# First loads of a fused attention and feed-forward kernel: keys and first queries first, and products of ones on TensorE while they load

## Chip, core and metric

The kernel runs on one core of a Trainium2 chip. The metric is the device time of one execution in microseconds. The time before is the median of 9 runs; beside it stands one profiled execution, from which all times of single instructions come.

## The reference

Attention over 8 batches of 8 heads, 576 tokens of 64 channels, in which a score counts only if it lies within tau of its row's maximum; the result, with heads side by side, goes through a gated feed-forward block. All is float32.

```
scores = (q @ k^T) / 8
scores = where(scores >= max(scores) - tau, scores, -1e9)
attn   = exp(scores - max) / (sum + 1e-9)
x      = (attn @ v) as (8*576, 512)
g      = x @ w_gate                       # 512 x 1536
out    = (g * sigmoid(g) * (x @ w_val)) @ w_out   # 1536 x 512
```

Weights arrive as they are in HBM; the kernel keeps w_gate and w_val in `wgv` and w_out in `wo`.

## The kernel before

**Work units.** Two heads make a pair; `NP` = 4 pairs make a batch, 32 pairs are done in all. A pair's queries and keys come as `[128, 18, 32]` tiles of 576 columns (`qraw`, `kraw`), are turned by VectorE's 32x32 transpose (`prepare`, L783 and L784) and multiplied. Queries are scaled first (L248, on GpSimd) with `scl`, which is computed from tau (L97 to L100).

**Segments.** The main loop runs over segments, numbered from 0, and in each over tiles of 128 queries. Segments 0 to 3 take the first two tiles (256 queries, `QA`) of pairs 0 to 3. Segments 4 to 7 take the other tiles (two of 128 and one of 64) of pairs 3, 0, 1, 2. From segment 8 on each segment is a whole pair in another layout. For segments 4 to 7 the remaining 320 queries of pairs 0 to 3 are transposed apart: pair 0's and pair 3's at L789 in `prepare`, pairs 1's and 2's at L856, at the end of the first two tiles of segment 4 (list `later`).

**A tile.** TensorE makes the scores (L311); VectorE takes the row maxima (L338); ScalarE takes exponentials (L345); VectorE cuts by tau and sums (L349), then L373 and L374 give the reciprocal. In segments 0 to 3 ScalarE scales an identity by it (L385), and TensorE turns the tile by multiplying with that (`flip`, L417, L420). In segments 4 to 7 the tile is scaled itself, head 0 on ScalarE (L357) and head 1 on GpSimd (L355), and TensorE transposes it (L415, L422). ScalarE copies the turned tile from PSUM (L423, L428); one tile later TensorE multiplies it with the values (`attend_tile`, L443).

**Weights.** A weight piece is loaded (`fetch_weights`) into a landing place, split by ScalarE (`split_weights`, L193, L194) and joined by VectorE (L200, L204, L207) and GpSimd (L209) in `join_weights`: 24 pieces, usually one in a tile, and a place can be loaded anew once its join is done. `need(n)` joins at once what products need.

**Feed-forward products.** They start in segment 4 and are dealt out between the attention steps: `pace` works out how many fit, `fill` issues them (gate L505 `pg`, value L505 `pv`).

**Order.** The schedule is manual: each engine, and each engine's DMA queue, works through its instructions in program order. SyncE's queue (SP) issues nearly all loads, ScalarE's the keys of pairs 0 and 1. The tile pool `ld` has one buffer each for `qraw` and `kraw`; pairs 1 and 2 use parts of `extra` instead. In segments 0 to 3 the next pair but one is fetched after `prepare`; from segment 4 on `fetch_qk(seg["i"] + 1)` stands in each segment's first tile, ahead of the steps that cut and scale that tile:

```python
            if x == 0 and n >= NP:
                fetch_qk(seg["i"] + 1)
            next(go)
```

Pair 4 is fetched in segment 2, since `n < NP` there and pair 3 is already loaded.

Of the kernel before, what the change touches and what calls it, by code (L numbers as in the profile page):

```python
# [10 lines left out]
F32 = mybir.dt.float32  # L11
U32 = mybir.dt.uint32
U64 = mybir.dt.uint64
AF = mybir.ActivationFunctionType
ALU = mybir.AluOpType
# [4 lines left out]
def kernel(  # L20
# [30 lines left out]
    nc = tc.nc  # L51
    P = 128
    B, H, S, D = q.shape
    NP = H // 2
# [3 lines left out]
    G = 32  # L58
    NG = P // G
    NJ = S // G  # L60
# [6 lines left out]
    TC = 256  # L67
    XB = 5
# [5 lines left out]
    QA = TA * P  # L74
    SCALE = 1.0 / float(D) ** 0.5
    assert 2 * D == P and NCC == NP and D == 2 * G and S - SM == 2 * G and SM % TC == 0 and B % BT == 0 and QA == TC

    const = ctx.enter_context(tc.tile_pool(name="const", bufs=1))
# [14 lines left out]
    cut = const.tile([P, 1], F32, name="cut")  # L93
    cap = const.tile([P, 1], F32, name="cap")
    scl = const.tile([P, 1], F32, name="scl")
    nc.sync.dma_start(out=tau_s, in_=tau.partition_broadcast(P))
    nc.vector.tensor_scalar(out=scl, in0=tau_s, scalar1=0.0, scalar2=SCALE, op0=ALU.is_ge, op1=ALU.mult)  # L97
    nc.vector.tensor_scalar(out=cap, in0=tau_s, scalar1=0.0, scalar2=2e38, op0=ALU.is_ge, op1=ALU.mult)
    nc.vector.tensor_scalar(out=cap, in0=cap, scalar1=-1e38, scalar2=None, op0=ALU.add)
    nc.vector.scalar_tensor_tensor(out=cut, in0=tau_s, scalar=-1.0, in1=cap, op0=ALU.mult, op1=ALU.min)  # L100


    sums = deque(const.tile([P, 4, 3], F32, name=f"sums{i}") for i in range(4))
    for x in sums:
        nc.vector.memset(x[:, :, 2], 1e-9)
    minus2 = const.tile([P, 1], F32, name="minus2")
    nc.vector.memset(minus2, -2.0)
    vall = const.tile([P, 2 * NJ * D], F32, name="vall")


# [4 lines left out]
    ident = pall.rearrange("p n s -> p (n s)")[:, free:free + P]  # L115
    make_identity(nc, ident)
    arenas = [pall[:, 0:NR, :], pall[:, NR - 2:, :]]

    wgv = const.tile([P, 2, NCC, DFF], F32, name="wgv")

# [49 lines left out]
    def fetch_weights(n=1):  # L170
        for _ in range(n):
            if not wpieces or wpieces[0][2] in used:
                return
            dst, srcs, place = wpieces.popleft()
            used.add(place)
            m = 2 if len(srcs) == 2 else nf
            to = places[place].bitcast(U64).rearrange("p (m n) -> p m n", m=m)
            if len(srcs) == 1:
                nc.sync.dma_start(out=to, in_=srcs[0])
            else:  # L180
                for x, src in enumerate(srcs):
                    nc.sync.dma_start(out=to[:, x, :], in_=src)
            fetched.append((dst, place))
# [43 lines left out]

    def load_qk(i):
        b, hp_ = divmod(i, NP)
        raws = []  # L230

        free = {1: 0, 2: 1}.get(i)
        for name, src, order in (("q", q, "(j r) (e d) -> e r j d"), ("k", k, "(j r) (e d) -> e r j d" if b == 0 else "(r j) (e d) -> e r j d")):
            if free is None:
                raw = ld.tile([P, NJ, G], F32, name=f"{name}raw")
            else:
                n = 2 * free + len(raws)
                raw = extra[:, n * S:(n + 1) * S].rearrange("p (j d) -> p j d", d=G)
            queue = nc.scalar if i < 2 and name == "k" else nc.sync

            for js in [slice(0, QA // G), slice(QA // G, NJ)] if i == 0 and name == "q" else [slice(0, NJ)]:
                for g in range(NG):
                    h, e = divmod(g, 2)
                    queue.dma_start(out=raw[g * G:(g + 1) * G, js],
                                    in_=src[b, 2 * hp_ + h].rearrange(order, r=G, d=G)[e][:, js])
            raws.append(raw.rearrange("p j d -> p (j d)"))
        for cs in [slice(0, QA), slice(QA, S)] if i == 0 else [slice(0, S)]:
            nc.gpsimd.tensor_scalar(out=raws[0][:, cs], in0=raws[0][:, cs], scalar1=scl, scalar2=None, op0=ALU.mult)  # L248
        return raws

    def load_v(seg):
        b, hp_ = divmod(seg["i"], NP)
        src = v[b, 2 * hp_:2 * hp_ + 2]
        if seg["halved"]:
            half = seg["i"] % 2
            vr = vall[:, half * NJ * D:(half + 1) * NJ * D].rearrange("p (h j d) -> p h j d", h=2, d=D)
            for a in range(2):
                for c in range(2):
                    nc.sync.dma_start(out=vr[(2 * a + c) * G:(2 * a + c + 1) * G].rearrange("r h j d -> r h (j d)"),
                                      in_=src.rearrange("h (r c j) d -> c r h (j d)", c=2, j=NK)[c])  # L260
        else:
            own = vall[:, hp_ * S:(hp_ + 1) * S]
            vr = own[:, 0:2 * KT * D].rearrange("p (h t d) -> p h t d", h=2, d=D), own[:, 2 * KT * D:]
            for h in range(2):
                nc.sync.dma_start(out=vr[0][:, h], in_=src[h, 0:KM].rearrange("(t p) d -> p t d", p=P))
                nc.sync.dma_start(out=vr[1][h * D:(h + 1) * D], in_=src[h, KM:S])
        seg["v"] = vr
# [493 lines left out]
        return rate  # L761

    raws = {}
    kept = {}
    later = []

    def fetch_qk(i):
        if i < NPAIR and i not in raws and i not in kept:
            raws[i] = load_qk(i)

    def prepare(seg):

        i = seg["i"]
        if i in kept:
            seg.update(kept[i])
            return
        qr, kr = raws[i]
        kept[i] = None
        qT = qkp.tile([P, S], F32, name="qT")
        if i < NP:  # L780
            kT = pall[:, 4 + i, :]
            rest = flat[:, i * (S - QA):(i + 1) * (S - QA)]
            nc.vector.transpose(out=kT, in_=kr)  # L783
            nc.vector.transpose(out=qT[:, 0:QA], in_=qr[:, 0:QA])  # L784

            later.append((rest, qr[:, QA:S]))
            if i == 1 or i == NP - 1:
                to, fr = later.pop(0 if i == 1 else -1)
                nc.vector.transpose(out=to, in_=fr)  # L789
            kept[i] = {"kT": kT, "qT": rest, "q0": QA}  # L790
        else:
            kT = qkp.tile([P, S], F32, name="kT")
            nc.vector.transpose(out=kT, in_=kr)
            nc.vector.transpose(out=qT, in_=qr)
        seg.update(kT=kT, qT=qT, q0=0)

    def give(n):
# [2 lines left out]
            left[0] += cost(u)  # L800
        gains[n] = (gains[n][0], 0)

    fetch_qk(0)
    prepare(segs[0])
    fetch_qk(1)
    fetch_weights(2)
    load_v(segs[0])
    fetch_weights(2)
    prev, last = None, iter(())
    for n, seg in enumerate(segs):  # L810
        if NP <= n < 2 * NP:
            seg["v"] = segs[seg["i"]]["v"]
        for x, t in enumerate(seg["tiles"]):
            go = scores(seg, t)
            next(go)
            next(last, None)
            attends = prev is not None and x == 1
            products = iter(())
            attend_tile()
            next(go)  # L820
            next(last, None)
            flip()
            if n == NP and x == 0:
                attend_tile()
                give(n - 1)
            if n == 2 * NP and x == 1:
                give(n - 1)
            if attends and n > 2 * NP:
                if prev["i"] % NP == 0:
                    need(NW)  # L830
                    start_batch(prev["i"] // NP)
                products = attend(prev)
            part = pace(n, x) / 2
            more = len(split)
            if n or x:
                split_weights()
                fetch_weights(2)
            if x == 0 and n >= NP:
                fetch_qk(seg["i"] + 1)
            next(go)  # L840
            double = t == NT and NP <= n < NP + 2
            if more and not double:
                join_weights()
            fill(part)
            next(go)
            fill(part)
            if double:

                join_weights(2)
                split_weights()  # L850
                fetch_weights(2)
            gates()
            last = go
            if n == NP and later:
                to, fr = later.pop(0)
                nc.vector.transpose(out=to, in_=fr)  # L856
            if attends and n > 2 * NP:
                next(products)
                next(products)
                give(n - 1)  # L860
            if attends and seg["halved"]:
                load_v(seg)
            if x == 0 and 0 < n < NP:
                load_v(seg)
            if x == len(seg["tiles"]) - 2 and n + 1 < len(segs):
                prepare(segs[n + 1])
                if n < NP:
                    fetch_qk(segs[n + 1]["i"] + 1)
        prev = seg
    next(last)  # L870
    next(last)
# [40 lines left out]
```

## Time and profile before

| what | us |
|---|---|
| median of 9 runs (lowest, highest) | 1514.29 (1512.86, 1515.15) |
| the profiled execution: its own time | 1514.79 |
| its span | 1512.7 |
| TensorE busy in the span | 1480.6 |
| VectorE busy | 994.8 |
| ScalarE busy | 726.4 |
| GpSimd busy | 642.6 |
| first scores start | 7.94 |
| scores of segments 0 to 3 (two tiles each) start | 7.94, 12.98; 20.63, 26.10; 32.16, 38.40; 45.01, 52.81 |
| segment 4's first scores start | 58.33 |

Span times count from the first instruction. In a line of the timeline the first number is the start, the second the length in us, then come engine, source line, operation, what is written from what, shape, count, and in brackets the idle time before it and who ended it. SPq and ACTq are the DMA queues of SyncE and ScalarE. A 32-bit product of 256 columns shows as two records.

### The profile page before, as it was taken

To read this page: it belongs to the slowest core of one execution; us is meant where nothing else is said; L and a number is where in the kernel's file an instruction comes from. 1 tells how busy PE (TensorE), PEld (TensorE's weight loads), DVE (VectorE), ACT (ScalarE), POOL (GpSimd) and SP (SyncE) were. 2 spreads that over 40 slices of the span, in tenths; PEclk is the share of its full clock that TensorE was granted. 3 is DMA by queue.
4 is the path that set the end of the run, shared out by engine and by line. 5 is a ranking of instruction groups with operands and counts; after the bars stand their busy time and mean duration, and the time that the engine had idled before them with its cause. 6 is when DMAs were issued, how large, how long until landed. Compare 5 with 4: busy or idle time off the path is not lost. (4 is left out here: it accounts for less than half of the span.)

```text
span 1512.7 us, 31439 instructions
## 1 busy us (share of the span) xinstructions
PE 1480.6 (98%) x11784; PEld 1123.1 (74%) x11784; DVE 994.8 (66%) x3038; ACT 726.4 (48%) x2157; POOL 642.6 (42%) x638
## 2 busy tenths in 40 slices
PE   7999899999999999999999999999999999999999
PEld 5777664477777777787777777777777777888887
DVE  6878988777777777747767666776666767512212
ACT  5787665555455555434545444454544454311110
POOL 3355543367454535336444444543545353500000
PEclk9999999999999999999999999999999999999999
DMA  8542411211112111112111111212110120000000
GB/s 192 149 147 92 96 35 39 54 33 32 47 33 47 33 25 33 40 28 45 35 27 29 25 47 33 46 33 47 33 35 13 46 48 16 1 15 1 15 14 15
DMA packets 176871, 66.91 MB, mean 44 GB/s; under 512 B 159696, under 2 KB 159696, under 8 KB 176720
## 3 DMA queue, kind: packets, MB, share of 16 engines
q1 hardware_dynamic: 169552, 56.45, 16.5%
q0 software_dynamic: 2432, 7.87, 1.4%
q8 instruction: 93, 1.52, 0.4%
q10 hardware_dynamic: 4736, 0.59, 0.3%
q14 instruction: 58, 0.48, 0.1%
HBM read 55.44 MB, written 9.44 MB: 43 GB/s over the span
## 5 line engine op out<-in xcount | busy, mean ns | idle before, releaser
L355 POOL TENSOR_SCALAR pall<-pall,ri 128x288 f32<-128x288 f32 (+1 forms) x260 | 265.2, 1029 | 345.3 <-DVE ri L365 308.8
L505 PE MATMUL pv<-xall,wgv 128*128 128x256 f32 x1728 | 405.0, 383 | 3.0 <-ACT pall L423 2.7
L505 PE MATMUL pg<-xall,wgv 128*128 128x256 f32 x1728 | 403.3, 383 | 0.2 <-ACT pall L423 0.2
L505 PEld LDWEIGHTS pv<-xall,wgv 128*128 128x128 f32 x1728 | 324.8, 191 | 68.5 <-issue 22.3
L505 PEld LDWEIGHTS pg<-xall,wgv 128*128 128x128 f32 x1728 | 324.0, 190 | 64.9 <-issue 22.0
L326 DVE TENSOR_REDUCE mx<-sc 128x2 f32<-128x576 f32 x252 | 180.6, 751 | 237.6 <-PE sc L303 236.8
L349 DVE SCALAR_TENSOR_TENSOR pall<-sc,th,pall 128x288 f32<-128x288 f32 (+1 forms) x540 | 258.1, 528 | 31.5 <-ACT pall L345 31.5
L345 ACT ACTIVATE pall<-sc,nm 128x288 f32<-128x288 f32 (+1 forms) x540 | 236.4, 510 | 0.6
L341 ACT ACTIVATE th<-nm,cut 128x4 f32<-128x4 f32 (+1 forms) x140 | 41.6, 297 | 383.6 <-DVE nm L330 383.6
L537 POOL TENSOR_TENSOR ht<-ht,gt 128x512 f32<-128x512 f32 x84 | 107.0, 1274 | 193.5 <-DVE ht L525 109.8
L394 DVE STREAM_TRANSPOSE pall<-pall 128x576 f32<-128x576 f32 x252 | 181.3, 754 | 2.8 <-POOL pall L355 2.8
L603 PE MATMUL po<-wo,ht 128*128 128x256 f32 x768 | 177.6, 382 | 0.0
L303 PE MATMUL sc<-kT,qT 64*32 64x288 f32 x4032 | 158.4, 411 | 11.3 <-DVE pall L349 9.9
L603 PEld LDWEIGHTS po<-wo,ht 128*128 128x128 f32 x768 | 144.9, 190 | 26.2 <-issue 6.0
L525 DVE SCALAR_TENSOR_TENSOR ht<-tn,pv 128x512 f32<-128x512 f32 x102 | 69.9, 685 | 132.3 <-PE pv L505 119.1
L357 ACT ACTIVATE pall<-pall,ri 128x288 f32<-128x288 f32 (+1 forms) x264 | 132.9, 553 | 0.0
L279 ACT COPY sums<-sums 32x4 f32<-32x4 f32 (+1 forms) x560 | 108.5, 194 | 50.0 <-DVE pall L349 38.6
L518 ACT ACTIVATE tn<-pg 128x512 f32<-128x512 f32 x108 | 64.9, 600 | 139.8 <-PE pg L505 133.0
L469 PE MATMUL xa<-pall,vall 64*64 64x288 f32 x2016 | 128.7, 405 | 0.0
L303 PEld LDWEIGHTS sc<-kT,qT 64*32 64x32 f32 x4032 | 58.9, 106 | 88.9 <-issue 60.9
L469 PEld LDWEIGHTS xa<-pall,vall 64*64 64x64 f32 x2016 | 74.5, 133 | 50.5 <-ACT sums L279 3.6
L621 POOL TENSOR_TENSOR ht<-ht,xall 128x256 f32<-128x256 f32 x48 | 34.1, 728 | 156.3 <-PE po L603 155.1
(101 smaller groups left out, 1329.5 us busy)
## 6 DMA issues: line engine op xcount, KB each, us to landing
vall<-in_v_dram SPq DMA_DIRECT2D x112, 144.0 KB, 3.3
qraw<-in_q_dram SPq DMA_DIRECT2D x116, 72.0 KB, 2.4
kraw<-in_k_dram SPq DMA_DIRECT2D x116, 72.0 KB, 2.8
out_dram<-ob POOLq DMA_DIRECT2D x28, 256.0 KB, 3.1
wo<-in_moe_w_gate_dram SPq DMA_DIRECT2D x16, 384.0 KB, 3.7
wo<-in_moe_w_val_dram SPq DMA_DIRECT2D x16, 384.0 KB, 4.3
xall<-in_moe_w_out_dram SPq DMA_DIRECT2D x5, 768.0 KB, 4.6
wo<-in_moe_w_out_dram SPq DMA_DIRECT2D x3, 768.0 KB, 4.5
```

Source lines behind the costliest of these rows:

```text
L279: nc.scalar.copy(out, in_[:, :, 0])
L303: nc.tensor.matmul(ps[g * G:(g + 1) * G, h, 0:SH], qT[hs, col + a * G:col + (a + 1) * G], kT[hs, c * SH:(c + 1) * SH], start=True, stop=True)
L326: nc.vector.tensor_reduce(out=mx[:, 2 * x:2 * x + 2, 0], in_=tile_[:, :, 0:SH], axis=AX.X, op=ALU.max, negate=True)
L345: nc.scalar.activation(ps[x], scs[x], AF.Exp, bias=nm[:, x:x + 1])
L349: nc.vector.scalar_tensor_tensor(out=ps[x], in0=scs[x], scalar=th[:, x:x + 1], in1=ps[x], op0=ALU.is_ge, op1=ALU.mult, accum_out=sm[:, x, ...
L355: nc.gpsimd.tensor_scalar(out=ps[x], in0=ps[x], scalar1=ri[:, x:x + 1], scalar2=None, op0=ALU.mult)
L357: nc.scalar.activation(ps[x], ps[x], AF.Copy, scale=ri[:, x:x + 1])
L394: nc.vector.transpose(out=p, in_=p)
L469: nc.tensor.matmul(xa[a][h * D:(h + 1) * D, at:at + n * G].rearrange("d (i q) -> d i q", q=G), vr[rs, h, j, :], p[rs, lo:lo + n, j, :], st ...
L505: nc.tensor.matmul(ps[:, i], wgv[:, mat, c, (f + i) * P:(f + i + 1) * P], x[:, c, cs], start=(c == 0), stop=(c == NCC - 1))
L537: eng.tensor_tensor(out=hts[x], in0=hts[x], in1=gt, op=ALU.mult)
L603: nc.tensor.matmul(ps, h(f), w[:, f, :], start=(f == 0), stop=(f == NF2 - 1))
```

## The change

- **Loads of the first four pairs.** Keys come first, then only the first 256 queries; each is four DMAs. For pairs 0 and 1 two of the four go on SP's queue and two on ScalarE's. Tau is loaded on ScalarE's queue behind pair 0's keys. Values of pair 0 are loaded ahead of pair 2 and of the weights, and pairs 2 and 3 are fetched before the main loop.
- **Rests.** The other 320 queries are loaded and scaled in the first tiles of segments 1 (pairs 3 and 0), 2 (pair 1) and 3 (pair 2).
- **Scaling.** Pair 0's first queries are scaled by VectorE, after its key transpose.
- **Places.** Pair 3's tiles are in `xall` instead of the `ld` buffers. Pair 4, next to use those, is now fetched by the line shown above, in segment 4's first tile; there the last reader of pair 0's `qraw`, the transpose of its rest, stands at the end of the same tile (`later` holds pairs 0, 1 and 2, one in each tile of segment 4).
- **Products of ones.** `run_idle(6)` issues six 128x128 by 128x256 products before everything else and six after the first tile's scores.
- **Weights.** The first piece is split in segment 1's first tile instead of segment 0's second, so joins 1 to 8 are one tile later.
- **A one-element exponential** stands ahead of ScalarE's first real work.

```diff
-    nc.sync.dma_start(out=tau_s, in_=tau.partition_broadcast(P))
-    nc.vector.tensor_scalar(out=scl, in0=tau_s, ...)
...
+    ones = pall[:, 2 * NR - 4, 0:TC]
+    nc.vector.memset(ones, 1.0)
+    def run_idle(n):
+        ps = ps_f.tile([P, 512], F32, name="idle", tag="psf")[:, 0:TC]
+        for _ in range(n):
+            nc.tensor.matmul(ps, ones[:, 0:P], ones, start=True, stop=True)
...
+        places_ = {1: extra[:, 0:2 * S], 2: extra[:, 2 * S:4 * S], 3: xall[:, XB * XW:XB * XW + 2 * S]}
...
+        def load(name, js, queues):
+            src, order = srcs[name]
+            for g in range(NG):
+                h, e = divmod(g, 2)
+                queues[g // 2].dma_start(out=tiles[name][g * G:(g + 1) * G, js],
+                                         in_=src[b, 2 * hp_ + h].rearrange(order, r=G, d=G)[e][:, js])
+        def scale(cs):
             nc.gpsimd.tensor_scalar(out=raws[0][:, cs], in0=raws[0][:, cs], scalar1=scl, ...)
+        if i < NP:
+            queues = [nc.sync, nc.scalar if i < 2 else nc.sync]
+            load("k", slice(0, NJ), queues)
+            if i == 0:
+                nc.scalar.dma_start(out=tau_s, in_=tau.partition_broadcast(P))
+            load("q", slice(0, QA // G), queues)
+            if i == 0:
+                nc.vector.tensor_scalar(out=scl, in0=tau_s, ...)
...
+            else:
+                scale(slice(0, QA))
+            def load_rest():
+                load("q", slice(QA // G, NJ), [nc.sync] * 2)
+                scale(slice(QA, S))
+            more_loads.append(load_rest)
+        else:
+            for name in "qk":
+                load(name, slice(0, NJ), [nc.sync] * 2)
+            scale(slice(0, S))
...
             nc.vector.transpose(out=kT, in_=kr)
+            if i == 0:
+                nc.vector.tensor_scalar(out=qr[:, 0:QA], in0=qr[:, 0:QA], scalar1=scl, ...)
             nc.vector.transpose(out=qT[:, 0:QA], in_=qr[:, 0:QA])
             later.append((rest, qr[:, QA:S]))
-            if i == 1 or i == NP - 1:
-                to, fr = later.pop(0 if i == 1 else -1)
+            if i == NP - 1:
+                to, fr = later.pop()
                 nc.vector.transpose(out=to, in_=fr)
...
+    run_idle(6)
     fetch_qk(0)
     prepare(segs[0])
     fetch_qk(1)
+    nc.scalar.activation(junk, minus2, AF.Exp)
+    load_v(segs[0])
+    fetch_qk(2)
     fetch_weights(2)
-    load_v(segs[0])
+    fetch_qk(3)
     fetch_weights(2)
...
             next(go)
+            if not n and not x:
+                run_idle(6)
             next(last, None)
...
-            if n or x:
+            if 0 < n < NP and x == 0:
+                if n == 1:
+                    more_loads.rotate(1)
+                    more_loads.popleft()()
+                more_loads.popleft()()
+            if n:
                 split_weights()
                 fetch_weights(2)
...
                 prepare(segs[n + 1])
-                if n < NP:
-                    fetch_qk(segs[n + 1]["i"] + 1)
```

More of the change, by code (lines that the diff above doesn't have):

```diff
@@ L95 @@
     scl = const.tile([P, 1], F32, name="scl")
-    nc.sync.dma_start(out=tau_s, in_=tau.partition_broadcast(P))
[L97 to L100, printed above, removed]
     sums = deque(const.tile([P, 4, 3], F32, name=f"sums{i}") for i in range(4))
@@ L107 @@
     nc.vector.memset(minus2, -2.0)
+    junk = const.tile([P, 1], F32, name="junk")
     vall = const.tile([P, 2 * NJ * D], F32, name="vall")
@@ L229, in load_qk @@
         b, hp_ = divmod(i, NP)
[L230 to L235, printed above, removed]
-            else:
[L237 to L246, printed above, removed]
@@ L247, in load_qk @@
-        for cs in [slice(0, QA), slice(QA, S)] if i == 0 else [slice(0, S)]:
-            nc.gpsimd.tensor_scalar(out=raws[0][:, cs], in0=raws[0][:, cs], scalar1=scl, scalar2=None, op0=ALU.mult)
+        tiles = {}
+        places_ = {1: extra[:, 0:2 * S], 2: extra[:, 2 * S:4 * S], 3: xall[:, XB * XW:XB * XW + 2 * S]}
+        srcs = {"q": (q, "(j r) (e d) -> e r j d"),
+                "k": (k, "(j r) (e d) -> e r j d" if b == 0 else "(r j) (e d) -> e r j d")}
+        for x, name in enumerate("qk"):
+            if i in places_:
+                tiles[name] = places_[i][:, x * S:(x + 1) * S].rearrange("p (j d) -> p j d", d=G)
+            else:
+                tiles[name] = ld.tile([P, NJ, G], F32, name=f"{name}raw")
@@ new lines, in load_qk @@
+        raws = [tiles[name].rearrange("p j d -> p (j d)") for name in "qk"]
+        def load(name, js, queues):
[5 more added lines that the diff above has]
+        def scale(cs):
+            nc.gpsimd.tensor_scalar(out=raws[0][:, cs], in0=raws[0][:, cs], scalar1=scl, scalar2=None, op0=ALU.mult)
@@ new lines, in load_qk @@
+        if i < NP:
[5 more added lines that the diff above has]
+            if i == 0:
+                nc.vector.tensor_scalar(out=scl, in0=tau_s, scalar1=0.0, scalar2=SCALE, op0=ALU.is_ge, op1=ALU.mult)
+                nc.vector.tensor_scalar(out=cap, in0=tau_s, scalar1=0.0, scalar2=2e38, op0=ALU.is_ge, op1=ALU.mult)
+                nc.vector.tensor_scalar(out=cap, in0=cap, scalar1=-1e38, scalar2=None, op0=ALU.add)
+                nc.vector.scalar_tensor_tensor(out=cut, in0=tau_s, scalar=-1.0, in1=cap, op0=ALU.mult, op1=ALU.min)
+            else:
[8 more added lines that the diff above has]
+            scale(slice(0, S))
@@ L763 @@
     raws = {}
+    more_loads = deque()
     kept = {}
@@ L783, in prepare @@
             nc.vector.transpose(out=kT, in_=kr)
+            if i == 0:
+                nc.vector.tensor_scalar(out=qr[:, 0:QA], in0=qr[:, 0:QA], scalar1=scl, scalar2=None, op0=ALU.mult)
             nc.vector.transpose(out=qT[:, 0:QA], in_=qr[:, 0:QA])
             later.append((rest, qr[:, QA:S]))
-            if i == 1 or i == NP - 1:
-                to, fr = later.pop(0 if i == 1 else -1)
+            if i == NP - 1:
+                to, fr = later.pop()
                 nc.vector.transpose(out=to, in_=fr)
```

## Prediction, before the result was known

> **What bounds the kernel now.** I read first the page's busy shares and slices, then busy time by stretches of 100 us, then the timeline of the first 95 us, then TensorE's granted clock microsecond by microsecond.
>
> The stretches (columns: stretch, its length, busy PE, PEld, DVE, ACT, POOL with instruction counts, PEclk, DMA share, GB/s):
>
> ```profile
> 0.00:100.00 100.00, 85.62 (x621) 63.76 (x621) 74.40 (x160) 71.23 (x148) 39.27 (x29) 0.98 0.64 161
> 100.00:200.00 100.00, 91.13 (x785) 66.14 (x785) 84.12 (x216) 72.21 (x167) 56.56 (x38) 0.98 0.35 96
> ...
> 300.00:400.00 100.00, 100.00 (x879) 75.64 (x872) 73.28 (x237) 52.18 (x168) 60.23 (x58) 1.00 0.14 30
> ```
>
> From about 300 us on TensorE never stops, and its work there isn't touched. So what the first 100 us gain or lose arrives at the end one for one; the change can reach at most the 14 us in which TensorE is idle there, plus the time in which it runs at half speed.
>
> The start, from the timeline:
>
> ```profile
> 6.78 0.78 DVE L783 STREAM_TRANSPOSE pall<-kraw 128x576 f32<-128x576 f32 x1 [2.72 <-DMA kraw<-in_k_dram]
> 7.48 0.40 DVE L784 STREAM_TRANSPOSE qT<-qraw 128x256 f32<-128x256 f32 x1
> ...
> 7.94 2.30 PE L311 MATMUL sc<-pall,qT 64*128 64x288 f32 x8 [7.94 <-DVE qT L784]
> ...
> 12.98 3.07 PE L311 MATMUL sc<-pall,qT 64*128 64x288 f32 x8 [2.75 <-DVE pall L349]
> ...
> 20.63 1.25 PE L311 MATMUL sc<-pall,qT 64*128 64x288 f32 x8
> ```
>
> The first scores wait for keys that land at 6.78. The same eight records take 2.30 us there and 1.25 us at 20.63: TensorE starts at half clock, though PEclk shows 1.00.
>
> After that VectorE sets the pace of the first eight tiles. Its first reduction of tile (segment 1, second) starts at 29.48, and the following tiles at 35.18, 42.33, 48.46, 54.59 and 60.67: steps of 5.7 to 7.2 us in which it hardly rests.
>
> Segment 4 (segments counted from 0; 58 to 82 us) is where the change adds a wait:
>
> ```profile
> 41.94 0.47 DVE L789 STREAM_TRANSPOSE pall<-qraw 128x320 f32<-128x320 f32 x1
> ...
> 42.47 1.96 SPq L244 DMA_DIRECT2D qraw<-in_q_dram  x4
> ...
> 46.63 2.08 POOL L248 TENSOR_SCALAR qraw<-qraw,scl 128x576 f32<-128x576 f32 x1 [3.67 <-DVE wgv L200]
> ```
> ```profile
> 64.61 1.87 POOL L355 TENSOR_SCALAR pall<-pall,ri 128x576 f32<-128x576 f32 x1 [1.90 <-DVE ri L374]
> ...
> 66.82 0.50 DVE L856 STREAM_TRANSPOSE pall<-extra 128x320 f32<-128x320 f32 x1
> ...
> 70.33 1.09 PE L415 MATMUL tp<-pall 128*128 128x128 f32 x8
> ```
>
> First fence: one load of queries (pair 4) has to wait for the last reader of the single qraw buffer; from that reader's end (42.41) to the scaled queries (48.71) 6.3 us pass. Second: L355, POOL's share of normalising a tile, is what TensorE's transposes at 70.33 read.
>
> **What the Trainium skill says.** *TensorE: Matmul & The Clock Gate*, "Part 1: The HAM clock gate", has TensorE start at half clock and change it at the ends of free-running windows of about 3.4 us, up after a busy window, down after an idle one. The trace agrees: the clock was 0.5 from about 47.1 to 50.6 and from 170.0 to 173.4, on one grid of 3.41 us, after idle stretches of 0.8 and 2.6 us. *DMA: Bandwidth & Descriptors*, "Issuing engines are not separate DMA queues", says that a second issuing engine saves only issue time. Here two queues issue one DMA per 0.45 us each, and eight were out by 3.1 us when the ninth waited until 4.02.
>
> **The change part by part.** A is the start of the first scores, 7.94 now.
>
> *Loads.* Before, the fourth key DMA was held until 4.36 and landed at 6.78; transposes of 0.78 and 0.40 gave 7.94. After, four keys, tau and four query pieces are nine DMAs. Eight go out by about 2.5; the ninth, a query piece on ACT's queue, waits as the ninth did before (4.02) and lands 2.0 (the shortest of L244) to 2.4 later, near 6.2. Tau, third on ACT's queue at about 1.7, lands 2.6 later as now: 4.4; the four small VectorE operations take 0.6, the key transpose 0.78, done by 5.9. Then the scaling on VectorE, 256 columns against 0.54 for 768 at L200, so 0.25, and 0.40: A is 6.9. **Gain 1.0**, bounds 0.2 (the ninth lands a microsecond later) and 1.7 (it isn't held).
>
> *Products of ones.* Sixteen records of 256 columns take 3.45 us in eight products, so one is 0.43, or 0.86 at half clock. Six from 1.2 us on end by 6.4, within the load wait. If they raised the clock, the first scores take 1.3 instead of 2.3. The second six (2.6) lie from A+1.3 to A+3.9. The next scores need their PSUM buffer back, 1.75 + 0.82 after the reduction starts (10.26 to 12.83 now), which is A+3.9 as well: cost nothing. Those scores end at A+5.4, the eight-record groups of the flip take 1.16 and 0.43 twice instead of 2.07, 0.69, 1.74, 0.43, with gaps until A+8.8, and segment 1's first scores come at A+8.9, now A+12.7. **Gain 3.8.** But 5.2 us of products hold a whole 3.4 us window only in half of the phases; if not, first scores and second products run slow: up to 2 us lost. I take 0.5.
>
> *Weights later.* Without the split in tile (0,1), tile (1,0) has no join on VectorE (0.54 + 0.56 + 0.96), and 0.47 of transposing the rest of pair 0's queries is gone too. Segment 1's second scores follow 5.5 later (the fastest step shown, 20.63 to 26.10) at A+14.4, its reduction at A+15.7, now A+21.5 (29.48). So 5.8 instead of 3.8 are gained there: **2.0 more**. From there VectorE paces both kernels with the same work, so by segment 4 the gain is 1.0 + 3.8 + 2.0 = **6.8**, less 0.5.
>
> *Pair 4's queries.* They were fetched in segment 2; now in the first tile of segment 4, ahead of L355 in POOL's order. Their buffer is pair 0's, and its last reader is the transpose of pair 0's rest, now put off to the end of that same tile (where L856 is at 66.82). So: end of that transpose 66.9 (no POOL beside the join before it), last of four issues 1.5 later, landing 2.0 to 2.7 later, scaling 1.7 to 2.1, and only then L355, 1.87: done near 74.7 instead of 66.5. TensorE's flip of that tile does head 0 (70.33 to 70.9) and stands until 74.7. Queued behind: this tile's weight add on POOL (needed two tiles later), and on TensorE the products of the first gate. A 1.4 us wait of TensorE at 73.37 on a PSUM copy falls away, so the pv products there start at 76.6 instead of 73.4. **Loss 3.3**, bounds 2.3 and 4.5. A gap of 3.8 us also drops the clock for one or two windows: 1.7 to 2.5, **loss 2.0**, bounds 0 and 3.4.
>
> *The put-off join.* Joins 1 to 8 are each one tile later, but gate 2, in the third tile of segment 4, needs eight: the eighth is forced there, ahead of the two done there anyway. VectorE has 2.1 + 0.47 more in that tile, and ScalarE's second split waits for POOL's third add (it already waited 2.81 us for one at 87.01). I put the exponentials of the next tile at 89.6 instead of 88.25; TensorE's scores at 90.14 have 0.33 us of slack at most. **Loss 1.2**, bounds 0 and 2.6.
>
> *At nothing:* twelve more DMA issues, about 5 us of SP, which waits for joins most of this time; the rests' POOL scalings (1.08 each), beside adds of 1.8 in tiles of 6 us; the early table load (1.28, now done at 9.07, needed at 11.05); pair 3's raw tile in xall; the DMA bytes, unchanged in sum, with the values' load now ahead of the weights'. If this cover is gone each costs under 1 us.
>
> Sum: -6.8 + 0.5 + 3.3 + 2.0 + 1.2 = **+0.2**. The profiled execution took 1514.79 (span 1512.7 and 2.1 around it), 0.5 above the median of 1514.29; so 1514.5 is the forecast. About 0.2%, 3 us, can be told from no change, so the borders are 1511.3 and 1517.3.
>
> **The rivals.** *The start's gain stays* (faster): the q4 wait is shorter or hidden, the clock holds and the late join finds slack: -6.8 + 2.3 + 0.5 = -4, some 1510.3. For it: DMA traffic at 67 us is lighter than at 42 us. Against it: three engines are near 90% busy there, and L355 is on TensorE's path with 4 us of slack, no more. *POOL's queue decides* (slower): the pair-4 load in front of L355 costs 4.5, the clock 3.4 and the join 2.6, together 10.5, against a start worth 5 with a late warm-up: +5.5, 1520. It decides once the wait at the flip plus the slow clock exceed about 8 us. For it: the same load took 6.3 us in this very trace. *The products don't raise the clock at all*: then the second six cost 5.2 at half clock in place of a 2.6 us gap, 2.5 lost and 3.4 not gained: about +6, 1520; against it the grid above, since TensorE is busy from A on.
>
> **How the numbers follow.** Gain and loss of nearly one size: 0.48 for about the same (own range 1511.3 to 1517.3), 0.25 for the first rival, 0.27 for the two slower ones (0.22 and 0.05). The range is 1509.5 to 1519.0.
>
> **What would show it.** First scores near 6.9 and in 1.3 us; segment 1's first scores near 15.8; segment 4's near 52, 6 to 7 us earlier than 58.33; then TensorE waiting 3 to 4 us on POOL L355 at its L415 transposes, SP waiting on the L789/L856 transpose before the qraw load, PEclk at 0.5 next. No such wait, or a gain at segment 4 under 4 us, would prove the sum wrong.

## The result, and the profile after

The changed kernel takes 1522.94 us (median of 9 runs, 1522.48 to 1525.09) against 1514.64 for the kernel before on the same chip: ratio 1.0056, interval 1.0048 to 1.0065. It is 8.3 us slower, where 0.2 was forecast; 1519.0 was the top of the range. The profiled execution took 1524.69 with a span of 1522.9, so in spans the loss is 10.2. That execution lies 1.75 above its kernel's median, the profiled one of before only 0.15 above its own: about 1.6 us of what the two profiles differ by belong to these executions.

The stretches of 100 us of the kernel after (columns as in the same view of before):

```profile
0.00:100.00 100.00, 84.61 (x566) 63.87 (x567) 68.76 (x144) 63.10 (x134) 33.41 (x27) 0.92 0.60 152
...
300.00:400.00 100.00, 99.24 (x905) 72.30 (x912) 71.03 (x237) 54.12 (x175) 59.69 (x58) 1.00 0.14 29
```

TensorE is busy in the first 100 us for almost as long as before (84.6 and 85.6), but 8.1 of it are the twelve products of ones (5.22 for the first six, 2.86 for the second), PEclk fell from 0.98 to 0.92, and VectorE, ScalarE and GpSimd each did 5.6 to 8.1 us less. The work of the front part is late; from 300 us on hardly anything differs. How late it is, is read from the start of each tile's scores. A tile (n,x) is tile x of segment n, both counted from 0; a gain is before less after.

| scores of tile | before | after | gain |
|---|---|---|---|
| (0,0) | 7.94 | 7.69 | 0.25 |
| (1,0) | 20.63 | 16.53 | 4.1 |
| (2,0) | 32.16 | 28.28 | 3.9 |
| (2,1) | 38.40 | 41.98 | -3.6 |
| (4,0) | 58.33 | 59.44 | -1.1 |
| (4,1) | 69.04 | 70.33 | -1.3 |
| (4,2) | 76.16 | 82.05 | -5.9 |
| (5,0) | 82.82 | 88.71 | -5.9 |
| (5,1) | 90.14 | 101.04 | -10.9 |

Up to (1,0) the gain, 4.1, is near the forecast 4.8. Then three steps of 7.5, 4.6 and 5.0 us follow, and 2.5 come back in between. The waits of TensorE in the first 320 us name one for each step (who waits, for what: us in total, times, longest):

```profile
PE xa L473 <- DMA vall<-in_v_dram: 5.4, 2, 5.0
PE pv L535 <- ACT xall L479: 4.0, 1, 4.0
PE tp L445 <- POOL pall L385: 3.3, 1, 3.3
```

The greatest such wait of TensorE's products is left out here: 10.0 in eleven times in segments with the other layout, which the kernel before has as well (9.9). L385 is the L355 of before, L445 the L415, L473 and L479 are the L443 and L449. With each gap TensorE falls to half clock, from about 33 to 40, 74 to 81 and 98 to 102. In the view by single microseconds PEclk is the third number from the end:

```profile
80.00:81.00 1.00, 1.00 (x4) 0.73 (x4) 0.00 (x0) 0.86 (x2) 1.00 (x1) 0.50 0.69 68
```

At the start, in the timeline:

```profile
5.52 0.15 DVE L263 TENSOR_SCALAR scl<-tau_s 128x1 f32<-128x1 f32 x1 [4.25 <-DMA tau_s<-in_tau_dram]
...
6.14 0.78 DVE L814 STREAM_TRANSPOSE pall<-kraw 128x576 f32<-128x576 f32 x1
...
7.69 1.25 PE L341 MATMUL sc<-pall,qT 64*128 64x288 f32 x8 [1.15 <-DVE qT L817]
...
16.53 1.95 PE L341 MATMUL sc<-pall,qT 64*128 64x288 f32 x8
```

The first scores take 1.25 instead of 2.30: six products of ones raised the clock in time.

The first step lies in SP's queue (SPq; the length of a group is from its first issue to the end of its last):

```profile
15.12 3.17 SPq L249 DMA_DIRECT2D xall<-in_k_dram  x4
...
18.33 4.77 SPq L249 DMA_DIRECT2D xall<-in_q_dram  x4
...
25.06 1.94 SPq L249 DMA_DIRECT2D xall<-in_q_dram  x4
...
27.04 4.76 SPq L249 DMA_DIRECT2D qraw<-in_q_dram  x4
...
31.84 0.46 SPq L295 DMA_DIRECT2D vall<-in_v_dram  x1
...
34.56 0.66 PE L473 MATMUL xa<-pall,vall 128*64 128x128 f32 x2 [4.95 <-DMA vall<-in_v_dram]
```

The values of pair 1 are needed at 29.6 (34.56 less 4.95) and issued at 31.84. In the kernel before they went out at 23.12 (timeline):

```profile
23.12 0.50 SPq L265 DMA_DIRECT2D vall<-in_v_dram  x1
```

Ahead of them SP now issues pair 3's eight loads, the four loads of two weight pieces at 23.14 to 25.0, and the rests of pairs 3 and 0, one behind the other without a pause. Four small loads take 4.8 us instead of 1.9 there. Meanwhile the data path isn't full: from 20 to 24 us the DMA share is 0.51 and 67 GB/s, before 1.21 and 175.

The second step is in segment 4, the third in segment 5:

```profile
67.69 0.50 DVE L902 STREAM_TRANSPOSE pall<-qraw 128x320 f32<-128x320 f32 x1
...
68.22 1.95 SPq L249 DMA_DIRECT2D qraw<-in_q_dram  x4
...
72.09 1.72 POOL L253 TENSOR_SCALAR qraw<-qraw,scl 128x576 f32<-128x576 f32 x1 [8.10 <-DMA qraw<-in_q_dram]
...
73.79 1.72 POOL L385 TENSOR_SCALAR pall<-pall,ri 128x576 f32<-128x576 f32 x1
...
75.57 1.11 PE L445 MATMUL tp<-pall 128*128 128x128 f32 x4 [3.29 <-POOL pall L385]
```
```profile
89.80 2.00 POOL L212 TENSOR_TENSOR wgv<-wgv,extra 128x768 uint32<-128x768 uint32 x1 [8.43 <-DVE wgv L210]
...
91.83 1.04 ACT L197 ACTIVATE extra<-wo,minus 128x768 f32<-128x768 uint32 x1 [1.75 <-POOL wgv L212]
...
94.17 4.16 POOL L212 TENSOR_TENSOR wgv<-wgv,extra 128x768 uint32<-128x768 uint32 x2 [2.37 <-DVE wgv L210]
...
96.59 0.99 ACT L197 ACTIVATE extra<-wo,minus 128x768 f32<-128x768 uint32 x1 [2.90 <-POOL wgv L212]
...
97.47 0.26 ACT L479 COPY xall<-xa 128x128 f32<-128x128 f32 x1
...
97.78 3.32 PE L535 MATMUL pv<-xall,wgv 128*128 128x256 f32 x8 [3.98 <-ACT xall L479]
```

The first fence is the chain that the prediction wrote down. In the second, the put-off join comes first, and two more weight pieces are joined in the same tile. ScalarE's first split (L197) has to wait until GpSimd's add (L212) of the put-off piece has let go of `extra`; its next one waits in the same way for the first of the two other adds. The copy L479, which TensorE's value products need, stands behind that split in ScalarE's order. The kernel before joins two pieces in this tile as well, and its split waits 2.81 us, but its adds start 1.77 us after the scores of (5,0) and not 5.46, and its value products wait next to nothing:

```profile
88.21 1.99 PE L505 MATMUL pv<-xall,wgv 128*128 128x256 f32 x8 [0.30 <-ACT xall L449]
```

### The profile page after: what moved, and what is told of

It reads as the page before. It is cut to its first block, busy times and chain, and to the rows that moved or that the text cites. A ratio compares the mean times of both kernels' runs of the same rounds, so it can differ in the third digit from the quotient of the medians.

```text
span 1522.9 us, 31512 instructions
## 1 busy us (share of the span) xinstructions
PE 1489.2 (98%) x11808; PEld 1130.4 (74%) x11808; DVE 998.0 (66%) x3040; ACT 726.8 (48%) x2158; POOL 642.5 (42%) x640
## 5 line engine op out<-in xcount | busy, mean ns | idle before, releaser
L535 PE MATMUL pv<-xall,wgv 128*128 128x256 f32 x1728 | 408.2, 385 | 5.2 <-ACT xall L479 4.0
L385 POOL TENSOR_SCALAR pall<-pall,ri 128x288 f32<-128x288 f32 (+1 forms) x260 | 265.2, 1029 | 338.1 <-DVE ri L395 314.0
L535 PE MATMUL pg<-xall,wgv 128*128 128x256 f32 x1728 | 403.6, 383 | 0.0
L535 PEld LDWEIGHTS pv<-xall,wgv 128*128 128x128 f32 x1728 | 327.2, 192 | 71.3 <-issue 22.3
L535 PEld LDWEIGHTS pg<-xall,wgv 128*128 128x128 f32 x1728 | 324.3, 190 | 64.4 <-issue 22.0
L333 PE MATMUL sc<-kT,qT 64*32 64x288 f32 x4032 | 158.3, 411 | 11.3 <-DVE pall L379 10.0
```

Of the source, the lines that this page charges most:

```text
L333: nc.tensor.matmul(ps[g * G:(g + 1) * G, h, 0:SH], qT[hs, col + a * G:col + (a + 1) * G], kT[hs, c * SH:(c + 1) * SH], start=True, stop=True)
L385: nc.gpsimd.tensor_scalar(out=ps[x], in0=ps[x], scalar1=ri[:, x:x + 1], scalar2=None, op0=ALU.mult)
L535: nc.tensor.matmul(ps[:, i], wgv[:, mat, c, (f + i) * P:(f + i + 1) * P], x[:, c, cs], start=(c == 0), stop=(c == NCC - 1))
```

## The experiments

Times are medians, ratios are to the kernel before on the same chip, with the 95% interval. Diffs are against the kernel after unless another is named. The kernel after stands at 1.0056 in that measure.

### Values ahead of the rests

```diff
             if 0 < n < NP and x == 0:
+                load_v(seg)
                 if n == 1:
...
-            if x == 0 and 0 < n < NP:
-                load_v(seg)
```

> The changed kernel with one edit: in the first tile of segments 1 to 3 the values are loaded ahead of the rests of the queries instead of at the tile's end. Theory (three added waits sum up): TensorE's 5.4 us wait on the values at 34.56 goes, and with it two half-speed windows (33.3 to 40.1); first scores of segment 4 come near 53 instead of 59.4, and the time falls from 1522.9 by 5.5 to 7, to 1516 to 1517.5. Rival (the wait is only moved, VectorE's joins set the pace anyway): under 2 us, above 1521.

Measured: 1521.47, ratio 1.0046 (1.0032 to 1.0061): 1.5 us less than the kernel after where 5.5 to 7 were expected, and with four runs and overlapping intervals that gain is not certain. The values now go out at 26.22, behind the weight pieces, and TensorE still waits for them (timeline):

```profile
32.63 0.59 PE L473 MATMUL xa<-pall,vall 128*64 128x128 f32 x2 [3.09 <-DMA vall<-in_v_dram]
```

The rests in front were only part of the delay. Pair 3 and the weights held SP too, and of the 5.6 us by which the values go out sooner only 1.9 arrive at TensorE: right behind the four weight loads (384 KB each) they take 5.6 to 6.3 us from issue to landing, in the kernel after 2.2 to 2.6. Segment 4 starts at 57.27 instead of 59.44.

### Values right behind pair 2

```diff
     fetch_qk(2)
+    load_v(segs[1])
     fetch_weights(2)
...
-            if x == 0 and 0 < n < NP:
+            if x == 0 and 1 < n < NP:
                 load_v(seg)
```

> The changed kernel with one edit: pair 1's values are loaded right behind pair 2's queries, ahead of the weights and of pair 3. Theory (their DMA is late because of what stands ahead of it on SP's queue): TensorE doesn't wait for them at all; but then the weight add behind the rests' scaling on POOL (34.43 now) holds ScalarE's split in segment 2's first tile by some 2 us, so segment 4's first scores come near 55 to 56.5 instead of 59.4, and the time is 1518 to 1520. Rival (the values were the one thing in segments 1 to 3): segment 4 near 52 to 53.5, 1515 to 1516.5.

Measured: 1520.40, ratio 1.0036 (1.0024 to 1.0048), just above the expected 1518 to 1520; segment 4 starts at 56.86. The wait on values is gone, and another has its place:

```profile
34.84 1.44 POOL L253 TENSOR_SCALAR xall<-xall,scl 128x320 f32<-128x320 f32 x1 [6.45 <-DMA xall<-in_q_dram]
...
36.26 1.22 POOL L253 TENSOR_SCALAR qraw<-qraw,scl 128x320 f32<-128x320 f32 x1
...
37.45 1.80 POOL L212 TENSOR_TENSOR wgv<-wgv,extra 128x768 uint32<-128x768 uint32 x1
...
39.28 0.98 ACT L197 ACTIVATE extra<-wo,minus 128x768 f32<-128x768 uint32 x1 [4.16 <-POOL wgv L212]
...
40.60 2.07 PE L447 MATMUL tp<-pall 128*128 128x128 f32 x8 [3.98 <-ACT pall L415]
```

Read upwards: TensorE's flip waits for ScalarE's scaled identity (L415), which stands behind a split (L197) that waits for GpSimd's weight add (L212), which stands behind the scaling of two rests (L253) whose loads come late. So the rests cost at two places, in SP's order and in GpSimd's. In the kernel after, TensorE's wait on values covers the second.

### Pair 4's queries at the end of segment 4's first tile

```diff
-            if x == 0 and n >= NP:
+            if x == 0 and n > NP:
                 fetch_qk(seg["i"] + 1)
...
+            if n == NP and x == 0:
+                fetch_qk(seg["i"] + 1)
```

The added lines stand behind the transpose of the rest.

> The changed kernel with one edit: pair 4's load and scaling are issued at the end of segment 4's first tile, after the transpose of pair 0's rest, so POOL L385 of that tile stands ahead of them. Theory: the 3.3 us wait of TensorE on L385 at 75.57 goes, and the clock stays at 1.0 there (two windows at half): 4.5 to 6 us less than 1522.9, 1517 to 1518.5. Rival (VectorE and ScalarE are late there anyway): about 2 us, 1521.

Measured: 1519.88, ratio 1.0036 (1.0022 to 1.0050), so 3.1 us, less than the 4.5 to 6 expected. TensorE's wait on L385 is gone, and PEclk is 1.00 from 74 to 81. The wait at L535 stays (3.96, now at 92.90), so it doesn't come from pair 4's load.

### No weight piece put off

```diff
-            if n:
+            if n or x:
                 split_weights()
```

> The changed kernel with one edit: the first weight piece is split in segment 0's second tile again, so that no join has to be forced in segment 4's third tile. Theory (the forced join makes ScalarE's splits wait for POOL's adds, and TensorE 4.0 us at 97.78): that wait shrinks to 0.3 as in the kernel before, 4 to 5.5 us less than 1522.9, 1517.5 to 1519; the join that comes back in segment 1 costs nothing here, since the wait on the values follows. Rival (the 4.0 us come from pair 4's load that put POOL's adds behind): no change, 1522 to 1523.5.

Measured: 1519.16, ratio 1.0031 (1.0020 to 1.0043), 3.8 us, a little less than the 4 to 5.5 expected. In the timeline the value products wait 0.31 instead of 3.98, and the L385 wait is untouched at 3.37:

```profile
92.58 1.99 PE L535 MATMUL pv<-xall,wgv 128*128 128x256 f32 x8 [0.31 <-ACT xall L479]
```

So the put-off join is the third step, and it is three times what the prediction gave it (1.2).

### All three together

The edits of the values ahead of the rests, of pair 4's queries and of the weight piece in one kernel.

> The changed kernel with the three edits of the other runs of this job together: values ahead of the rests, pair 4's load behind its buffer's last reader, first split in segment 0. Theory (the start's gain is real and the three waits hid it): TensorE waits none of the three times; segment 1's first scores at 16.5 and segment 4's near 54, about 4 us ahead of the kernel before; 1509 to 1511.5, that is 3 to 5.5 us less than before. Rival (the gain at the start is lost again in segments 1 to 3 whatever is done there): 1514 to 1515.5, no difference to before.

Measured: 1517.33, ratio 1.0019 (1.0011 to 1.0027); 5.6 us come back, above either theory's time. The three waits are gone or under 0.9, but a fourth has come (timeline):

```profile
38.46 0.99 ACT L197 ACTIVATE extra<-wo,minus 128x768 f32<-128x768 uint32 x1 [7.58 <-POOL wgv L212]
...
39.79 2.08 PE L447 MATMUL tp<-pall 128*128 128x128 f32 x8 [5.97 <-ACT pall L415]
```

It is the chain through GpSimd of the version with the values right behind pair 2, longer still, with PEclk at 0.51 from 38 to 45. To take waits away was not enough while the rests stood ahead of the weight adds.

### The rests at the ends of tiles

The three edits, and the rests moved behind the tile's joins:

```diff
             if 0 < n < NP and x == 0:
+                load_v(seg)
-                if n == 1:
-                    more_loads.rotate(1)
-                    more_loads.popleft()()
-                more_loads.popleft()()
...
+            if (n, x) in ((1, 0), (1, 1), (2, 1), (3, 0)):
+                more_loads.rotate((n, x) == (1, 0))
+                more_loads.popleft()()
```

> The three edits together, and the rests of the queries loaded and scaled one at a time at the ends of tiles (1,0), (1,1), (2,1) and (3,0), behind the tile's weight add, instead of ahead of it. Theory (POOL stands in the rests' scaling until their DMAs land, the weight add behind it keeps ScalarE's split waiting 7.58 us at 38.46, and TensorE 5.97 at 39.79): that wait goes with its two half-speed windows, and the time falls from 1517.3 to 1509.5 to 1512. Rival (SP's queue is so late that the values or the weights hold the same tile instead): 1515 to 1517.

Measured: 1511.68, ratio 0.9983 (0.9977 to 0.9990). This version beats both kernels: 11.3 us below the kernel after and 2.6 below the one before. Its stretches and its waits of TensorE up to 110 us (the latter without what stands ahead of the first scores):

```profile
0.00:100.00 100.00, 92.79 (x665) 69.46 (x666) 76.79 (x166) 73.59 (x155) 42.62 (x32) 1.00 0.66 166
```
```profile
PE sc L341 <- DVE pall L379: 2.1, 3, 0.9
PE pv L535 <- ACT pall L453: 1.4, 1, 1.4
...
PE xa L473 <- DMA vall<-in_v_dram: 0.3, 1, 0.3
```

No wait is longer than 1.4 us, the clock holds at 1.00, and segment 4's first scores start at 55.22, 3.1 before those of the kernel before. That lead stays to the end: (5,0) starts at 79.89, 2.9 ahead. Loads and scalings of the rests were moved together, so this run doesn't tell SP's order from GpSimd's.

### Tau and values further forward

The version above, with tau first on SP's queue, and with pair 1's values and two weight pieces (four loads) ahead of pair 3:

```diff
-                nc.scalar.dma_start(out=tau_s, in_=tau.partition_broadcast(P))
+                nc.sync.dma_start(out=tau_s, in_=tau.partition_broadcast(P))   # now ahead of the keys
...
     fetch_weights(2)
-    fetch_qk(3)
+    load_v(segs[1])
     fetch_weights(2)
+    fetch_qk(3)
```

> The same, and on SP's queue tau ahead of the keys, pair 1's values and four weight pieces ahead of pair 3's eight small loads. Theory (loads are limited by the order on SP's queue, and a gain at the start comes through once nothing later waits): first scores near 6.9 instead of 7.4 to 7.7, no wait of TensorE on values or ScalarE in segments 1 to 3, 1508 to 1510.5. Rival (the pace of VectorE from segment 1 on takes it back): 1513 to 1515, as before.

Measured: 1514.80, ratio 1.0003 (0.9995 to 1.0011), a miss by 4 us. Tau lands sooner, but the key transpose starts no sooner and the first scores start later (timeline):

```profile
3.48 0.15 DVE L263 TENSOR_SCALAR scl<-tau_s 128x1 f32<-128x1 f32 x1 [2.21 <-DMA tau_s<-in_tau_dram]
...
6.12 0.78 DVE L814 STREAM_TRANSPOSE pall<-kraw 128x576 f32<-128x576 f32 x1 [2.04 <-DMA qraw<-in_q_dram]
...
8.03 1.84 PE L341 MATMUL sc<-pall,qT 64*128 64x288 f32 x8 [1.98 <-DVE qT L817]
```

With tau ahead of them the other loads come later: the keys land 3.3 to 4.4 us after issue instead of 2.6 to 3.7, the queries 3.0 to 4.4 instead of 2.5 to 3.6, and SP's issues of both are later too. So the run doesn't show what an earlier tau alone would bring. The products of ones did raise the clock (a record takes 0.63 us at first and 0.38 from about 5 us on), but then TensorE stands 1.98 us for the queries, and half clock follows: PEclk is 0.57 from 8 to 12. In the kernel after that stand is 1.15 us, and the clock holds. And pair 3's scaling on GpSimd, now with a later load, stands ahead of the weight adds, with PEclk at 0.59 from 36 to 40.

### Products of ones alone, with and without

The kernel before with `run_idle(6)` at the two places and nothing else of the change (its ones are written by GpSimd):

> The kernel before with nothing but the twelve products of ones (set by GpSimd, six at the start, six after the first scores). Theory (half clock costs about 3.5 us until segment 1, and VectorE passes that on): 1510.5 to 1512, 2 to 4 us less than before. Rival (VectorE's pace or the loads swallow it): 1513.5 to 1515.

Measured: 1512.98, ratio 0.9994 (0.9986 to 1.0002). The scores of (1,0) start at 17.66 instead of 20.63, segment 4's at 56.42 instead of 58.33; of 3.0 us gained 1.9 reach segment 4, and at the end, where 2 to 4 were expected, no difference from before is certain.

The kernel after without them:

```diff
-    run_idle(6)
...
-            if not n and not x:
-                run_idle(6)
```

> The changed kernel without the products of ones. Theory (what they bring is swallowed in the changed kernel by the wait on pair 1's values, whose DMA is issued at 31.84 whatever TensorE does): segment 1's first scores 3 us later, but TensorE's wait at the values shorter by as much, and the time within 1.5 us of 1522.9. Rival (a gain at the start comes through one for one): 1525.5 to 1527.

Measured: 1522.18, ratio 1.0055 (1.0039 to 1.0070): as slow as the kernel after. (1,0) starts at 20.90, 4.4 later than with them, and then TensorE never waits for values. Those are issued at 29.67, only 2.2 earlier than in the kernel after, but are needed 4.0 later. Segment 4's first scores come at 56.80, 2.6 earlier than with the products. The L385 wait is there (3.34), and the one at L535 too (3.96). That the 2.6 us don't show in the time can lie in the profiled execution of the kernel after, 1.75 above its median; it stays open.

So in this change the products' 3.85 us go into the wait on values and its clock windows: TensorE comes sooner to a load that doesn't.

The version with the rests at the ends of tiles, without the products:

> The kernel with the three waits mended and the rests moved to the tiles' ends, but without the products of ones. Theory (at the start half clock costs 3.5 to 4 us until segment 1, and VectorE's pace gives most of that back, as in the kernel before with the products alone, where 1.1 us were left): 1512 to 1513.5, 0.5 to 2 us more than with them (1511.7). Rival (without late loads the start comes through in full): 1514.5 to 1515.5.

Measured: 1513.78, ratio 0.9993 (0.9987 to 1.0000). (1,0) starts at 20.76, segment 4 at 57.52. Where nothing waits behind them the products are worth 2.1 us by the medians and 1.5 by the ratios, the surer measure, since the two versions ran on different chips: within the 0.5 to 2 expected.

### The clock held up through the L385 wait

```diff
             for h in range(2):
+                if h == 1 and seg is segs[NP] and t == TA:
+                    idle = ps_f.tile([P, 512], F32, ...)[:, 0:P]
+                    for _ in range(14):
+                        nc.tensor.matmul(idle, ident, ident, start=True, stop=True)
```

The loop is the one over heads in `flip`.

> The changed kernel, and in segment 4 fourteen products of the identity with itself (128 columns, about 0.2 us each) between head 0's and head 1's transposes, where TensorE stands 3.3 us for POOL. Theory (that gap costs its length and a half-speed stretch of 6.8 us besides): the gap stays, the clock is 1.0 from 74 to 81, and the time falls by 2 to 3, to 1520 to 1521. Rival (VectorE and ScalarE set the end of those tiles, the slow clock is free): 1522 to 1523.5.

Measured: 1522.22, ratio 1.0042 (1.0028 to 1.0055). The extra products fill the wait, and the clock holds in the same microsecond as shown of the kernel after:

```profile
80.00:81.00 1.00, 1.00 (x18) 0.78 (x16) 0.66 (x1) 0.24 (x1) 1.00 (x1) 1.00 0.73 129
```

From (4,1) to (4,2) are 9.25 us instead of 11.72, so 2.5 of that step's 4.6 are the clock. That a gap brings the half clock and products in it prevent that is what the Trainium skill has in *TensorE: Matmul & The Clock Gate*, "Part 1: The HAM clock gate", and this trace agrees. But the page has the drop after at least one idle window of about 3.4 us, and here less was enough: half clock came with a wait of 3.29 us in the kernel after, and it followed a stand of 1.98 in the version with tau further forward and one of 0.8 in the kernel before, which the prediction took for agreement. Since it did not follow the stand of 1.15 us ahead of the first scores of the kernel after, the length of a gap alone doesn't decide. At the end less is certain: the median moved by 0.7, the ratio by 0.0014 or 2.1 us, with an interval of 2 us to each side. What the clock is worth in the total these runs don't settle.

## Why the prediction was wrong, step by step

All in us, minus is a gain; measured from the starts of the scores, the weights' step from VectorE's first reduction of (1,1), 29.48 before and 24.14 after. By the medians the sum is 8.3; the rest belongs to the two profiled executions, and in which steps it lies isn't known.

| step | predicted | measured |
|---|---|---|
| first loads | -1.0 | -0.25 |
| products of ones | -3.8, +0.5 set aside | -3.85 |
| weights later | -2.0 | -1.2 |
| from (1,1) to segment 4, "at nothing" and VectorE pacing | 0 | +6.4 |
| in segment 4's first tile, up to (4,1) | 0 | +0.2 |
| pair 4's queries: wait and clock | +3.3 and +2.0 | 4.6 in all |
| put-off join | +1.2 | +5.0 |
| after that | 0 | -0.7 |
| sum | +0.2 | +10.2 in spans |

**The step that failed is "at nothing: twelve more DMA issues, about 5 us of SP, which waits for joins most of this time".** From 13 to 32 us SP goes from one load to the next, and pair 1's values stand behind all of these. The loads that now stand ahead delay them by 8.7 us (23.12 to 31.84). The price of an issue failed too: 1.2 us (4.77 and 4.76 for four) in place of 0.45. In the second of these groups eight loads are out, and SP's queue waits three times, 2.8 us in all, for weight loads to land; the prediction had read this from the ninth load at the start and did not carry it on to here. In the first group no such wait is on record, and why single issues took 2.00 and 1.73 us is open. The kernel after pays 7.5 for it at (2,1), of which 2.5 come back by segment 4. The values right behind pair 2 and the kernel without products, in which this wait is gone, confirm the mechanism. The prediction's own sign of being wrong, a gain under 4 us at segment 4, came as a loss of 1.1.

**"The rests' POOL scalings, beside adds of 1.8 in tiles of 6 us" failed as well**, but hidden. Their 1.08 us were costed and the wait for their loads was not, 6.79 us at 32.32. GpSimd stands in it with a weight add behind, which ScalarE and then TensorE need. With the values early this is what ends TensorE's wait (3.98 and 5.97), and moving the rests behind the joins gained 5.6 us (1517.33 to 1511.68). The prediction asked that question for pair 4's load and not for the same kind of load in segments 1 to 3.

**The put-off join** was the right mechanism with a term mis-sized: 1.2, with bounds of 0 and 2.6, against a wait of 4.0 and a half-clock window, together 5.0. I had counted VectorE's 2.1 us and looked at the next tile's exponentials. What ended the wait was ScalarE's order: the put-off piece's add holds the first split for 1.75, the next split waits 2.90 for the first of the two other adds (2.39), and the copy L479 stands behind it.

**Pair 4's queries** came as written, link by link: transpose, issue, landing, scaling, L385, and a wait of 3.29 against 3.3. With the clock it is 4.6 against 5.3.

**The products of ones** came as forecast. The set-aside 0.5, for a clock that rises too late, was not needed: of ten profiles with them nine have first scores of 1.25 us, and in the tenth (tau further forward) the clock had risen and fell again in the stand before the scores. They are the part whose gain the late values ate.

**Tau and the first loads.** I had 6.9 for the first scores and 4.4 for tau; 7.69 and 5.5 came. Tau took 3.7 us to land and not 2.6. VectorE goes from the last operation on tau (5.95) to the key transpose (6.14) and on to the queries without a wait, so in this kernel tau held it and not the keys or the queries, and tau's landing is the term that was mis-sized. The scaling by VectorE took 0.31 against 0.25, the transpose of the queries 0.45 against 0.40.

**The rivals.** The slower ones stood at 1520, nearer than the forecast. But neither is what happened: L385's wait was not above its central value, and the products did raise the clock. Their size was near by other causes. The rival that was missing is "pair 1's values behind everything else on SP".

## To carry to other kernels

Before an added load is costed at nothing, write out the whole list of its issuing queue with issue times, and compare for each load behind it when it goes out and when it is needed; do the same for every in-order engine that gets a step that waits for a load. A load that goes out right behind big ones lands later, too. A gain at the start is worth nothing if the next resource has a fixed time of arrival: see first what comes in at that time. Several waits that cover each other are found only by taking them away together, since removing one (here the wait on values) shows the next.

## What the runs showed of the hardware that was not expected

- The same kind of load can take over twice as long to issue: the four `xall` query loads behind pair 3's keys took 4.77 us to issue, four slightly larger ones later 1.94 (both in the fence of SP's queue). Bandwidth stayed unused meanwhile: from 22 to 23 us, during an issue of 1.73 us, the DMA engines moved 4 GB/s.
- A load behind big ones lands late: with four weight loads of 384 KB right ahead of them, pair 1's values took 5.6 to 6.3 us from issue to landing, and 2.2 to 2.6 in the kernel after.
- A wait for a load on GpSimd reached TensorE through two other engines: 6.45 us there, 4.16 on ScalarE, 3.98 on TensorE.
- Six products of ones ahead of them gave first scores of 1.25 us in the kernel after, though TensorE then stood 1.15 us for the queries. Where it stood 1.98 us (tau further forward) the scores took 1.84 and half clock followed.
- A gap of 3.3 us in which TensorE is idle cost nearly as much again in clock: 2.5 of the 4.6 us of its tile.
